# Seven products of halves in place of eight in one product of a two-MLP kernel

## The chip, the cores and the metric

The kernel runs on one NeuronCore of a Trainium2 chip. The core has five engines with queues of their own: TensorE (PE; its weight loads are shown as PEld), VectorE (DVE), ScalarE (ACT), GpSimd (POOL) and SyncE (SP), which issues most DMAs. Matmuls write into PSUM, eight banks of 512 f32 values in each of 128 partitions; everything else works in SBUF. The metric is the device time of one execution in microseconds (us); of several executions the median is told.

## What is computed

```python
# q, k, v: (4, 8, 576, 64) f32
out_up    = repeat(softmax_attention(mean of 4 rows of q, k, v), 4)   # pooled attention
out_local = softmax(q k^T / 8 where |i - j| < 4) v                    # windowed attention
x = (out_up + out_local) as (2304, 512)

h = x @ w_in                                   # first MLP, 512 -> 2048 -> 512
x = np.maximum(0.01 * h, h) @ w_out

h = x @ w_in2                                  # second MLP, 512 -> 2048 -> 512
g = np.where(h >= 1, h, np.where(h <= -1, 0.0, (h + 1) ** 2 / 4))
out = g @ w_out2                               # (2304, 512) f32
```

## The kernel before

**Numbers.** Every operand of the four MLP products is held as two f16 parts, a high one and the rest (`hi`, `lo`). A product is made of three f16 products, hi x hi, hi x lo and lo x hi, that add up in PSUM.

**Tiling.** The 2304 tokens are cut into five blocks, `BLOCKS = [512, 512, 512, 512, 256]`. A stage is one MLP m and one block b, and `ORDER` lists the ten stages. A stage of 512 tokens has 16 steps, one for each tile f of 128 columns of d_ff; the 256-token block has 8 steps with two tiles each. A step is:

- `g1`: the first product of one f (two for block 4), 4 tiles of d_model x 3 = 12 matmuls of all the block's tokens (24 of 256 columns for block 4), into one PSUM bank.
- `act_a` to `act_l`: the activation out of the bank and the split into hi and lo. In the first MLP that is `act_a` and `act_h` on ScalarE and `act_l` on VectorE; in the second `act_a`, `act_s` (ScalarE), `act_g` (VectorE, it frees the bank), `act_h` (ScalarE) and `act_l` (VectorE).
- `g2`: the second product's share of that f, 12 matmuls that add up in the stage's up to four `acc` banks over all steps. Behind the last step `fin_*` evict them, and in the second MLP a DMA writes the result.

The weights are loaded by SyncE, converted by VectorE and ScalarE, and stay in SBUF (`w1`, `w2`). The space of `w2` serves as scratch (`w` in the trace) for the attention until the second MLP's weights come. All other buffers come from one arena.

**Attention.** Batch 0 and part of batch 1 go through TensorE (`prep`, `down`, `local_p`), the remaining units of 256 tokens through VectorE (`local_d`: products and sums over windows). `ADD_PE` lists the batches for which `local_p` adds the pooled attention by an f32 matmul with the identity into the bank (L1106); for the others VectorE adds it (`xa`).

**Order.** Nothing is ordered at run time. A planner in the kernel (`Issue.run`) goes through modelled time, and gives each free engine the ready operation with the lowest key; keys come from the step an operation is due in, less a lead. Gates limit what is open: a first product may start while under two (`h_open`) are open, and a stage's `acc` banks wait for those of the stage before. `QUEUE` is how far the planner lets SyncE issue ahead of the modelled DMAs, `lat` what it takes a DMA to cost. Up to 140 us it puts matmuls of zeros (`fill`, L1675) where TensorE would stand idle in its model. The instructions then stand in each engine's queue in that order, with semaphore waits between engines.

## Time and profile before

| | |
|---|---|
| median of 3 runs | 862.63 us (861.98 to 864.24) |
| profiled execution | 868.02 us, its span 866.2 us |
| TensorE busy, matmuls | 855.9 us, 5029 records |
| VectorE, ScalarE, GpSimd busy | 551.4, 386.2, 44.4 us |
| mean granted TensorE clock | 0.997 |
| DMA | 67.69 MB |

The span goes from the first to the last instruction; the run's time has a little around it. Matmuls are pipelined: a record runs until its result has left the array, so records overlap, and the spacing of their starts tells what one costs. In the profile DVE is VectorE and so on, `bank` is PSUM, `arena` and `w` are buffers in SBUF, and `<-` goes from what is read to what is written.

### The profile page before, as it was taken

The numbers are of one execution on the slowest core, as the hardware profiler recorded it, in microseconds if no ns is written. First come the engines' busy times: TensorE is split into PE (matmuls) and PEld (weight loads), VectorE is DVE, ScalarE is ACT, GpSimd is POOL, SyncE is SP. The second block draws the span as 40 slices with busy tenths as digits, with TensorE's granted clock in tenths as the row PEclk, the third lists the DMA queues.
The fourth block names the chain that finished last, engine by engine and source line by source line (L and its number), as shares of the span: only waits on it lengthen the run. The fifth ranks groups of instructions, "written<-read, shape, count | busy, mean of one in ns | idle before, by whom it ended". The sixth has DMA issues, their size and how long they took to land.

```text
span 866.2 us, 13124 instructions
## 1 busy us (share of the span) xinstructions
PE 855.9 (99%) x5029; PEld 440.8 (51%) x5039; DVE 551.4 (64%) x975; ACT 386.2 (45%) x909; POOL 44.4 (5%) x64
## 2 busy tenths in 40 slices
PE   9998999999999999999999999999999999999998
PEld 5764555444444444444444444444444488544564
DVE  5767999899999899569959928921323211322221
ACT  5858776364444334644453223222433332433343
POOL 2201000000000033001410000000000000000000
PEclk9999999999999999999999999999999999999999
DMA  7999574647720353321751002000000010000010
GB/s 133 183 156 206 183 220 151 219 137 221 219 92 2 110 82 69 98 76 28 119 136 43 1 30 81 1 0 1 1 1 1 0 50 1 1 1 1 1 50 25
DMA packets 80365, 67.69 MB, mean 78 GB/s; under 512 B 36398, under 2 KB 70062, under 8 KB 80302
## 3 DMA queue, kind: packets, MB, share of 16 engines
q1 hardware_dynamic: 69102, 62.69, 26.9%
q0 software_dynamic: 11200, 4.15, 4.3%
q8 instruction: 40, 0.66, 0.3%
q14 instruction: 23, 0.19, 0.1%
HBM read 62.08 MB, written 4.72 MB: 77 GB/s over the span
## 4 chain that ended last, share of the span: by engine, by line
PE 81%; DVE 7%; DMA 6%; issue 2%; ACT 2%; SPq 1%; POOL 0%; DVEq 0%; POOLq 0%; ACTq 0%
PE bank L1471 38%; PE bank L1536 21%; PE bank L1548 16%; DMA w<-in_v_dram 4%; DMA arena<-in_v_dram 2%; DVE arena L1322 1%; PE bank L962 1%; PE bank L944 1%; DVE arena L1515 1%; DVE arena L1499 1%; DVE arena L1292 1%; ACT w L1070 1%; PE bank L1112 1%; PE bank L893 1%; SPq L732 1%
## 5 line engine op out<-in xcount | busy, mean ns | idle before, releaser
L1471 PE MATMUL bank<-arena,w 128*128 128x512 f16 (+1 forms) x1920 | 396.9, 358 | 0.4 <-ACT arena L915 0.3
L1471 PEld LDWEIGHTS <-w 128*128 128x128 f16 x1920 | 186.8, 98 | 183.9 <-issue 2.8
L1536 PE MATMUL bank<-arena,w 128*128 128x512 f16 (+1 forms) x960 | 198.8, 358 | 0.2
L1548 PE MATMUL bank<-w,arena 128*128 128x512 f16 x864 | 198.5, 379 | 0.4 <-ACT arena L1511 0.2
L1515 DVE SCALAR_TENSOR_TENSOR arena<-arena 128x512 f16<-128x512 f32 x144 | 99.3, 690 | 122.6 <-ACT arena L1511 122.4
L1536 PEld LDWEIGHTS <-w 128*128 128x128 f16 x960 | 92.9, 98 | 91.5 <-issue 1.2
L1499 DVE SCALAR_TENSOR_TENSOR arena<-arena,bank 128x512 f32<-128x512 f32 x72 | 49.3, 685 | 135.2 <-ACT arena L1495 135.2
L1548 PEld LDWEIGHTS <-arena 128*128 128x128 f16 x864 | 83.7, 98 | 97.9 <-issue 1.0
L1511 ACT ACTIVATE arena<-arena 128x512 f16<-128x512 f32 x144 | 90.6, 629 | 74.1 <-DVE arena L1499 72.0
L1491 ACT ACTIVATE arena<-bank,half 128x512 f32<-128x512 f32 x72 | 49.4, 686 | 132.5 <-PE bank L1471 132.5
L1487 ACT ACTIVATE arena<-bank 128x512 f32<-128x512 f32 x72 | 42.9, 595 | 141.8 <-PE bank L1471 140.2
L1495 ACT ACTIVATE arena<-arena 128x512 f32<-128x512 f32 x72 | 45.3, 629 | 2.0
L1322 DVE TENSOR_TENSOR arena<-arena 128x768 f32<-128x768 f32 (+2 forms) x60 | 41.2, 689 | 1.5
L1247 DVE TENSOR_TENSOR arena<-arena 128x1792 f32<-128x1792 f32 x20 | 40.3, 2019 | 0.5 <-DMA arena<-in_k_dram 0.4
L1255 DVE TENSOR_REDUCE arena<-arena 128x28 f32<-128x1792 f32 x20 | 40.3, 2013 | 0.0
L1292 DVE TENSOR_TENSOR arena<-arena 128x1792 f32<-128x1792 f32 x20 | 40.2, 2016 | 0.0
L607 ACT ACTIVATE w<-arena 128x512 f16<-128x512 f32 x37 | 23.2, 629 | 35.8 <-DVE arena L591 35.5
L840 POOL DMA_DIRECT2D arena<-in_q_dram x8 | 10.4, 1296 | 300.1 <-DMA arena<-in_q_dram 233.6
L640 DVE SCALAR_TENSOR_TENSOR w<-arena,w 128x512 f16<-128x512 f32 x37 | 25.4, 692 | 0.1
L1675 PE MATMUL bank<-zeros 128*128 128x512 bf16 x65 | 20.9, 418 | 3.5 <-ACT w L1099 2.0
L584 DVE SCALAR_TENSOR_TENSOR arena<-arena 128x512 int32<-128x512 int32 x33 | 22.8, 694 | 0.1
L591 DVE SCALAR_TENSOR_TENSOR arena<-arena 128x512 int32<-128x512 int32 x33 | 22.8, 693 | 0.0
(132 smaller groups left out, 628.5 us busy)
## 6 DMA issues: line engine op xcount, KB each, us to landing
arena<-in_moe_w_out_dram SPq DMA_DIRECT2D x21, 512.0 KB
arena<-in_moe_w_in_dram SPq DMA_DIRECT2D x17, 512.0 KB
w<-in_moe_w_in_dram SPq DMA_DIRECT2D x15, 512.0 KB
w<-in_moe_w_out_dram SPq DMA_DIRECT2D x11, 512.0 KB
out_dram<-arena SPq DMA_DIRECT2D x18, 256.0 KB
arena<-in_k_dram SPq DMA_DIRECT2D x23, 112.0 KB
arena<-in_v_dram SPq DMA_DIRECT2D x23, 112.0 KB
w<-in_q_dram SPq DMA_DIRECT2D x14, 144.0 KB
```

Source lines behind the costliest of these rows:

```text
L1247: nc.vector.tensor_tensor(pv(par, j0), st["q", par].ap.rearrange("p (j d) -> p j d", d=D)[:, j0:j0 + JC, :] .unsqueeze(2).to_broadcast([P, ...
L1292: nc.vector.tensor_tensor(pv(par, j0), window(st["v", par], j0, JC), sv(par)[:, j0:j0 + JC, :].unsqueeze(3).to_broadcast([P, JC, W, D]), o ...
L1322: nc.vector.tensor_tensor(out, x, y, op=ALU.add)
L1471: nc.tensor.matmul(h[:, e], a[:, f, c, :], y[:, :, c, :], start=(n == 0), stop=(n == 3 * KDM - 1),)
L1487: nc.scalar.activation(out=t, in_=st["h", p], func=AF.Prelu, scale=s_in * sg, alpha=0.01)
L1491: nc.scalar.activation(out=t, in_=st["h", p], func=AF.Relu, scale=0.5 * s_in, bias=half)
L1495: nc.scalar.activation(out=t, in_=t, func=AF.Square, scale=s_in ** -0.5)
L1499: nc.vector.scalar_tensor_tensor(out=t, in0=t, scalar=1.0 / s_in, in1=st["h", p], op0=ALU.min, op1=ALU.max)
L1511: nc.scalar.activation(out=gv(p)[0], in_=st["t", p].ap, func=AF.Copy, scale=so)
L1515: nc.vector.scalar_tensor_tensor(out=lo, in0=st["t", p].ap, scalar=so, in1=hi, op0=ALU.mult, op1=ALU.subtract)
L1536: nc.tensor.matmul(o, a, y[:, e, :], start=(first and n == 0 and c % E == 0), stop=(last and n == 2), skip_group_check=True,)
L1548: nc.tensor.matmul(st["acc"][tt], a, y[:, f, :], start=(first and n == 0), stop=(last and n == 2),)
```

## The change

The first product of the second MLP, for token blocks 2, 3 and 4 (1280 tokens), is made by the seven-product scheme of Strassen in Winograd's form. d_model, d_ff and the block's tokens are each halved. Eight products of halves would be the plain way; seven are enough when sums of halves are multiplied. With weight quarters A(row half of d_ff, half of d_model) and token quarters B(half of d_model, half of the tokens):

- `weight_sums` makes S1 to S4 of the weight quarters for each f of the lower half of d_ff (`FH` = 8 tiles), once. VectorE adds, ScalarE makes the high part, VectorE the low part. S3 takes the place of quarter 21 in `w2`; this starts when the last plain stage of the second MLP, block 1, has used its weights.
- `token_sums` makes T1 to T4 of a block in the same way.
- A step now handles a pair, f and f+8 (two pairs of tiles at once in block 4), in two banks, one for each half of the tokens, each bank holding both d_ff halves. `s1` makes three products, ScalarE copies two of them out (`m5`, `m1`), `s2` adds two more products, ScalarE copies one sum (`m53`), VectorE adds into the banks (`d0`, `d1`), `s3` adds a product, VectorE adds (`d2`, which completes the second half of the tokens), `s4` adds the last one (the first half of the tokens is complete).
- A product of halves (`prod`) is 2 tiles of d_model x 3 = 6 matmuls over half the block's tokens: 256 columns in the 512 blocks; in block 4, where E = 2 tiles go together, 12 matmuls of 128 columns.
- The activation runs as before on a bank of 512 values, now for one half of the tokens and both f. The second product (`g2_half`) is made in groups of 6 matmuls of 512 columns for one half of the tokens and one f.

Beside that, stage (1, 4), the first MLP's 256-token block, goes ahead of (2, 2); `ADD_PE` is empty; `QUEUE` is 3, and the planner's `lat` of two kinds of loads differ.

```diff
 ORDER = [
     (1, 0), (1, 1), (2, 0), (2, 1), (1, 2), (1, 3),
-    (2, 2), (1, 4), (2, 3), (2, 4),
+    (1, 4), (2, 2), (2, 3), (2, 4),
 ]
+SEVEN = (2, 3, 4)
...
-QUEUE = 2
+QUEUE = 3
...
-ADD_PE = (0,)
+ADD_PE = ()
...
-        o = ch.op("SP", DMA, load, need=(1024,), lat=1.75)
+        o = ch.op("SP", DMA, load, need=(1024,), lat=(2.3, 1.6)[which])
...
+    def half_sums(ch, n, quarter, dst, recipe, deps, need):
+        st = {}
+        ready = {}
+        def make(name, x, y, sx, sy):
+            if name == recipe[0][0] and need:
+                need[1]()
+            qx = quarter(x)
+            if y in st:
+                st[name] = b = buf(n)
+                v = b.ap[:, 0:n]
+                if len(qx.shape) == 4:
+                    v = v.rearrange("p (a b) -> p a b", a=qx.shape[2])
+                st["v" + name] = v
+                f = st["v" + y]
+                if sx > 0:
+                    nc.vector.tensor_tensor(v, qx[:, 0], f, op=ALU.subtract)
+                    nc.vector.tensor_tensor(v, v, qx[:, 1], op=ALU.add)
+                else:
+                    nc.vector.tensor_tensor(v, f, qx[:, 0], op=ALU.subtract)
+                    nc.vector.tensor_tensor(v, v, qx[:, 1], op=ALU.subtract)
+            else:
+                st[name] = b = buf(2 * n)
+                a = b.ap.rearrange("p (k x) -> p k x", k=2)
+                if len(qx.shape) == 4:
+                    a = a.rearrange("p k (a b) -> p k a b", a=qx.shape[2])
+                nc.vector.tensor_tensor(a, qx, quarter(y), op=ALU.add if sy > 0 else ALU.subtract)
+                v = st["v" + name] = a[:, 0]
+                nc.vector.tensor_tensor(v, v, a[:, 1], op=ALU.add)
...
+        def lo(name):
+            d = dst(name)
+            nc.vector.tensor_tensor(d[:, 1], st["v" + name], d[:, 0], op=ALU.subtract)
...
+            h = ch.op("ACT", t_act(n), lambda name=name: hi(name), [o])
+            ready[name] = o = ch.op(
+                "DVE", t_dve(n), lambda name=name: lo(name), [h],
...
+    def weight_sums(f, due):
...
+            s_ap[f] = {"S1": a[:, 0], "S2": a[:, 1], "S4": a[:, 2], "S3": quarter("21")}
...
+        s_ready[f] = half_sums(
+            ch, HD, quarter, lambda nm: s_ap[f][nm],
+            (("S1", "21", "22", 1, 1), ("S2", "11", "S1", -1, 1), ("S4", "12", "S2", 1, -1),
+             ("S3", "11", "21", 1, -1)),
+            s_after[f], (words, make))
...
+    def token_sums(b, due):
...
+        t_ready[b] = half_sums(
+            ch, 2 * n, quarter, lambda nm: t_ap[b][nm],
+            (("T1", "12", "11", 1, -1), ("T2", "22", "T1", 1, -1), ("T4", "21", "T2", 1, -1),
+             ("T3", "22", "12", 1, -1)),
+            x2[b].ready, (KDM * tokens(b), make))
...
-                           need=(QBB * P,), lat=1.85)
+                           need=(QBB * P,), lat=1.95)
...
+        def prod(p, t, j, w, y, first=False):
+            o = part(p, t, j)
+            for e in range(E):
+                n = 0
+                for c in range(2):
+                    a = w(E * p + e).rearrange("p s (c n) -> p s c n", c=2)
+                    for i, k in ((0, 0), (0, 1), (1, 0)):
+                        nc.tensor.matmul(
+                            o[:, e], a[:, i, c], y[:, k, c, :],
+                            start=first and e == 0 and n == 0, stop=n == 5,
+                            skip_group_check=True,
+                        )
+                        n += 1
...
+        def s1(p, i):
+            sch.step = max(sch.step, i)
+            h_open[0] += 2
+            for t in range(2):
+                st["h", (p, t)] = banks.get(True)
+            prod(p, 1, 0, ws("S1"), t_ap[b]["T1"], True)
+            prod(p, 0, 1, wq(0, 0), xq(0, 0), True)
+            prod(p, 0, 0, wq(0, 1), xq(1, 0))
+        def side(p, nm):
+            return st[nm, p].ap[:, 0:E * NH].rearrange("p (a n) -> p a n", a=E)
+        def copy(p, nm, t, j):
+            st[nm, p] = buf(E * NH)
+            nc.scalar.copy(side(p, nm), part(p, t, j))
+        def s2(p):
+            prod(p, 1, 0, ws("S4"), xq(1, 1))
+            prod(p, 0, 1, ws("S2"), t_ap[b]["T2"])
+        def d0(p):
+            nc.vector.tensor_tensor(part(p, 0, 0), part(p, 0, 0), side(p, "m1"), op=ALU.add)
+        def d1(p):
+            nc.vector.tensor_tensor(part(p, 1, 0), part(p, 0, 1), side(p, "m53"), op=ALU.add)
+        def s3(p):
+            prod(p, 0, 1, ws("S3"), t_ap[b]["T3"])
+        def d2(p):
+            nc.vector.tensor_tensor(part(p, 1, 1), part(p, 0, 1), side(p, "m5"), op=ALU.add)
+        def s4(p):
+            prod(p, 0, 1, wq(1, 1), t_ap[b]["T4"])
...
+            def copied(nm, t, j, dep, p=p, key=key):
...
+            o1 = sch.add(
+                "PE", fn=lambda p=p, i=i: s1(p, i),
+                deps=x.ready + [w_ready[m, 0, f] for f in fs] + sr["S1"] + [tr["T1"]],
+                key=float(i), banks=2,
+                gate=lambda i=i: h_open[0] <= 2 and i < low_step[0] + LAGMAX, **unit(3),
+            )
+            m5 = copied("m5", 1, 0, o1)
+            m1 = copied("m1", 0, 1, o1)
+            o2 = sch.add("PE", fn=lambda p=p: s2(p),
+                         deps=[m5, m1, tr["T2"]] + sr["S4"] + sr["S2"], key=i + 0.2, **unit(2))
+            m53 = copied("m53", 1, 0, o2)
+            a0 = summed(d0, "m1", [o2])
+            a1 = summed(d1, "m53", [m53])
+            o3 = sch.add("PE", fn=lambda p=p: s3(p), deps=[a0, a1, tr["T3"]] + sr["S3"],
+                         key=i + 0.4, **unit(1))
+            a2 = summed(d2, "m5", [o3])
+            o4 = sch.add("PE", fn=lambda p=p: s4(p),
+                         deps=[a2, tr["T4"]] + [w_ready[m, 0, f + FH] for f in fs],
+                         key=i + 0.6, after=(x.s.done, t_buf[b].done) if p == PH - 1 else (),
+                         **unit(1))
+            halves.append((p, 1, i + 1, i + 2.5, a2))
+            halves.append((p, 0, i, i + 4.1, o4))
+        for p, t, i, key, o1 in halves:
+            fs = [E * p + e for e in range(E)]
+            ol = act((p, t), i, o1)
+            for j in range(2):
+                first = p == j == 0 and t == 1
+                og2 = sch.add(
+                    "PE", 3 * NACC // 2 * t_mm(512) * E,
+                    lambda p=p, t=t, j=j, i=i: g2_half(p, t, j, i),
+                    [ol, og2] + [w_ready[m, 1, f + FH * j] for f in fs],
...
     for m, b in ORDER:
+        if m == 2 and b in SEVEN:
+            if not s_ready:
+                for f in range(FH):
+                    weight_sums(f, first[m, b] + 2.0 * (f // per_step(b)))
+            token_sums(b, first[m, b])
         stage(m, b)
```

The places where the order differs, as far as a later step rests on it. On TensorE, in the second MLP's block 2, before: a first product of 12 matmuls into one bank, and then a second product of 12. `w_61` is the second MLP's weights, `bank_66` and the like are PSUM banks, and the arena holds the tokens and the activations.

```order
L1471 LDWEIGHTS w_61
L1471 MATMUL bank_65<-arena,w_61 128x512 [waits DVE_49]
...
L1471 MATMUL bank_65<-arena,w_61 128x512
L1548 LDWEIGHTS arena [waits Activation_49]
L1548 MATMUL bank_68<-w_61,arena 128x512
```

After, in the same block, the third pair: the end of its `s1` (L1626) with the second-product group (L1696) behind it, then `s2` into two banks, a second-product group, and the start of `s3`.

```order
L1626 LDWEIGHTS w_61
L1626 MATMUL bank_66<-arena,w_61 128x256
L1696 LDWEIGHTS arena [waits Activation_49]
L1696 MATMUL bank_70<-w_61,arena 128x512
...
L1626 MATMUL bank_69<-arena 128x256 [waits Activation_49]
...
L1626 MATMUL bank_66<-arena 128x256 [waits Activation_49]
...
L1696 LDWEIGHTS arena
L1696 MATMUL bank_70<-w_61,arena 128x512
...
L1626 LDWEIGHTS w_61
L1626 MATMUL bank_66<-arena,w_61 128x256 [waits DVE_49]
```

Where one first product and one second product of 12 matmuls took turns, a piece of 6 to 18 matmuls takes turns with a group of 6, and pieces that go on in a pair wait for ScalarE (`Activation`) or VectorE.

On VectorE in the same block, before, the two operations of the activation chain, L1499 and L1515, stand alone:

```order
L1499 SCALAR_TENSOR_TENSOR arena<-arena,bank_69 128x512 [waits PE_49,Activation_49]
L1515 SCALAR_TENSOR_TENSOR arena<-arena 128x512 [waits Activation_49]
L1499 SCALAR_TENSOR_TENSOR arena<-arena,bank_67 128x512 [waits PE_49,Activation_49]
L1515 SCALAR_TENSOR_TENSOR arena<-arena 128x512 [waits Activation_49]
L1499 SCALAR_TENSOR_TENSOR arena<-arena,bank_65 128x512 [waits PE_49,Activation_49]
```

After, one pair: the three adds into the banks (L1666, L1669, L1676) and the two activation chains (L1721, L1737).

```order
L1666 TENSOR_TENSOR bank_65<-bank_65,arena 128x256 [waits PE_49,Activation_49]
L1669 TENSOR_TENSOR bank_64<-bank_65,arena 128x256 [waits DVE_49,Activation_49]
L1676 TENSOR_TENSOR bank_64<-bank_65,arena 128x256 [waits DVE_49,PE_49]
L1721 SCALAR_TENSOR_TENSOR arena<-arena,bank_64 128x512 [waits DVE_49,Activation_49]
L1737 SCALAR_TENSOR_TENSOR arena<-arena 128x512 [waits Activation_49]
L1721 SCALAR_TENSOR_TENSOR arena<-arena,bank_65 128x512 [waits PE_49,Activation_49]
L1737 SCALAR_TENSOR_TENSOR arena<-arena 128x512 [waits Activation_49]
```

Three operations that wait for TensorE and for the copies of ScalarE have come between the chains.

On TensorE near 27 us, before: the f32 matmul of the pooled attention (L1106) in front of each group of the windowed one (L1112), with fill matmuls (L1675) between.

```order
L1106 MATMUL bank_66<-arena,ident 128x256 [waits Activation_49]
L1112 MATMUL bank_66<-w_61 64x64 [waits DMAHW0_49]
L1112 MATMUL bank_66<-w_61 64x64 [waits DMAHW1_49]
L1112 MATMUL bank_66<-w_61 64x64 x6
L1675 LDWEIGHTS zeros
L1675 MATMUL bank_63<-zeros 128x512
...
L1106 MATMUL bank_65<-arena,ident 128x256 [waits DVE_49]
```

After, the same place: L1238 is the windowed attention's product, L1964 the fill.

```order
L1964 LDWEIGHTS zeros
L1964 MATMUL bank_63<-zeros 128x512
L1238 MATMUL bank_70<-w_61 64x64 [waits DMAHW0_49,Activation_49]
L1238 MATMUL bank_70<-w_61 64x64 [waits DMAHW1_49]
L1238 MATMUL bank_70<-w_61 64x64 x6
L1964 LDWEIGHTS zeros
L1964 MATMUL bank_63<-zeros 128x512
L1238 MATMUL bank_65<-w_61 64x64 [waits DVE_49,Activation_49]
```

L1106 has gone, and its place is taken by a fill matmul or nothing; what it added is now added by VectorE.

## Rows read from the trace of the kernel before

**Rows 1.** The page, parts 1 and 2: busy time, and slices in tenths.

```profile
PE 855.9 (99%) x5029; PEld 440.8 (51%) x5039; DVE 551.4 (64%) x975; ACT 386.2 (45%) x909; POOL 44.4 (5%) x64
...
PEclk9999999999999999999999999999999999999999
```

**Rows 2.** The page, part 4: the chain that ended last, by engine and line.

```profile
PE 81%; DVE 7%; DMA 6%; issue 2%; ACT 2%; SPq 1%; POOL 0%; DVEq 0%; POOLq 0%; ACTq 0%
PE bank L1471 38%; PE bank L1536 21%; PE bank L1548 16%; DMA w<-in_v_dram 4%; DMA arena<-in_v_dram 2%; DVE arena L1322 1%; PE bank L962 1%; PE bank L944 1%; DVE arena L1515 1%; DVE arena L1499 1%; DVE arena L1292 1%; ACT w L1070 1%; PE bank L1112 1%; PE bank L893 1%; SPq L732 1%
```

**Rows 3.** The chain in time, two late pieces: start, length (us), what.

```profile
505.43 2.59 PE bank L1471 x12
...
718.95 2.62 PE bank L1471 x24
```

**Rows 4.** The chain in order of time, between 40 and 80 us.

```profile
44.23 7.73 DMA w<-in_v_dram
...
65.61 8.23 DMA w<-in_v_dram
77.94 3.64 PE bank L1471 x12
```

**Rows 5.** Groups by shape, weight loads: xcount, busy us, mean ns, idle.

```profile
L1471 PEld LDWEIGHTS <-w 128*128 128x128 f16 x1920 | 186.8, 98 | 183.9 <-issue 2.8 <-DVE w L577 0.3
...
L944 PEld LDWEIGHTS bank<-ident,w 72*72 72x72 f32 x64 | 5.4, 115 | 2.1 <-ACT w L915 0.2
```

**Rows 6.** Timeline at 336 us: start us, length us, engine, line, operation.

```profile
336.27 0.46 PEld L944 LDWEIGHTS bank<-ident,arena 72*72 72x72 f32 x4
...
336.48 0.42 PE L944 MATMUL bank<-ident,arena 72*72 72x72 f32 x4
...
336.73 0.38 PE L1548 MATMUL bank<-w,arena 128*128 128x512 f16 x1
```

**Rows 7.** Timeline, second MLP, block 2: the chain behind a first product.

```profile
684.85 2.75 PE L1548 MATMUL bank<-w,arena 128*128 128x512 f16 x12
685.05 0.69 ACT L1491 ACTIVATE arena<-bank,half 128x512 f32<-128x512 f32 x1 [2.45 <-PE bank L1471]
685.77 0.63 ACT L1495 ACTIVATE arena<-arena 128x512 f32<-128x512 f32 x1
686.43 0.69 DVE L1499 SCALAR_TENSOR_TENSOR arena<-arena,bank 128x512 f32<-128x512 f32 x1 [3.10 <-ACT arena L1495]
...
687.81 0.69 DVE L1515 SCALAR_TENSOR_TENSOR arena<-arena 128x512 f16<-128x512 f32 x1 [0.69 <-ACT arena L1511]
```

**Rows 8.** Groups by shape: 256-column copy and add out of a bank.

```profile
L780 ACT ACTIVATE w<-bank 128x256 f32<-128x256 f32 x16 | 6.1, 384 | 0.6 <-PE bank L767 0.6
...
L1342 DVE TENSOR_TENSOR arena<-bank,arena 128x256 f32<-128x256 f32 x4 | 1.5, 420 | 1.1 <-PE bank L1328 1.1
```

**Rows 9.** Timeline, the end of the program.

```profile
856.51 2.75 PE L1548 MATMUL bank<-w,arena 128*128 128x512 f16 x12
...
858.81 0.63 ACT L1511 ACTIVATE arena<-arena 128x512 f16<-128x512 f32 x1 [0.75 <-DVE arena L1499]
...
859.49 3.06 PE L1548 MATMUL bank<-w,arena 128*128 128x512 f16 x12 [0.23 <-ACT arena L1511]
```

**Rows 10.** Stretches (us): length, busy us of PE, PEld, DVE, ACT, POOL, clock, DMA.

```profile
460.00:515.00 55.00, 55.00 (x285) 26.62 (x284) 41.60 (x59) 17.64 (x40) 0.26 (x1) 1.00 0.00 1
515.00:560.00 45.00, 45.00 (x210) 20.42 (x209) 37.50 (x47) 13.37 (x24) 0.25 (x1) 1.00 0.18 53
560.00:610.00 50.00, 50.00 (x234) 22.66 (x232) 10.87 (x15) 11.94 (x20) 0.00 (x0) 1.00 0.00 0
```

**Rows 11.** Groups by shape: the f32 matmuls that add the pooled attention.

```profile
L1106 PE MATMUL bank<-arena,ident 128*128 128x256 f32 x16 | 5.4, 418 | 0.3 <-ACT arena L970 0.2 <-ACT w L780 0.2
```

**Rows 12.** Timeline of TensorE at 27 us.

```profile
26.85 0.69 PE L1106 MATMUL bank<-arena,ident 128*128 128x256 f32 x2 [0.16 <-ACT arena L970]
...
28.09 0.61 PE L1675 MATMUL bank<-zeros 128*128 128x512 bf16 x2
```

128 lines of the change are left out of this document (117 added, 11 removed).

## The prediction

> **What bounds the kernel now.** I read the page's first two parts first [rows 1]. TensorE is busy 855.9 us, 99% of the span, VectorE 551.4 and ScalarE 386.2, and the granted clock stands at 9 in every slice, the 2.4 GHz level. A busy share says little of pipelined matmuls, so the chain of work that ended last came next [rows 2]: 81% of it is TensorE, and its three long lines are the matmuls of the two MLPs (L1471 the first product, L1536 and L1548 the second). In order of time [rows 3] these pieces stand end to end: 12 matmuls of 512 columns take 2.59 us, 24 of 256 columns 2.62 us. So a matmul costs its columns, 216 ns and 109 ns from start to start, and no step waits for another. From about 78 us to the end the time is the sum of TensorE's work; before that the chain runs through DMAs of v [rows 4]. A change pays by the columns that it takes from TensorE after 78 us, less every gap that it opens there.
>
> The profiled execution took 868.0 us (span 866.2, 1.8 around it), 5.4 above the median of 862.6. The terms below are differences in that execution, and I take their sum off the median too.
>
> **Columns removed.** Token blocks 2 and 3 (512 tokens each) and 4 (256 tokens) of the second MLP change. Before, the first product of a 512 block is 16 steps of 12 matmuls of 512 columns, so two blocks are 384 x 0.216 = 82.9 us; block 4 is 192 matmuls of 256 columns, 192 x 0.109 = 20.9 us. Together 103.9 us. Afterwards a pair of column tiles (f and f+8) takes seven products of 6 matmuls over half the tokens each. Blocks 2 and 3: 2 x 8 pairs x 42 = 672 matmuls of 256 columns, 672 x 0.109 = 73.2 us. The second product keeps its 480 matmuls of 512 columns, now in groups of six.
>
> Block 4 becomes 4 pairs x 84 = 336 matmuls of 128 columns, each with a weight load of its own. No f16 matmul of 128 columns stands in the trace. From below: 216 less 109 ns for 256 columns is 0.418 ns a column, which gives 55.5 ns and 18.6 us in all. From above: a weight load of this form is recorded as 98 ns [rows 5], and if the matmuls come no faster than that, it is 32.9 us. I take 55.5, because the nearest row speaks for it: four f32 transposes of 72 columns take 0.25 us (336.48 to 336.73), 62 ns each, although each has a weight load of its own [rows 6], recorded as 115 ns [rows 5]. The recorded length of a load is a latency, not a spacing, and a load with a matmul can be issued every 62 ns. So the first product falls from 103.9 to 73.2 + 18.6 = 91.8 us, 12.1 less; with the upper price it would be 106.1, 2.2 more.
>
> Here the Trainium skill speaks against the change. Its page "TensorE: Matmul & The Clock Gate", section "Back-to-back issue gap", says that a stream of weight loads and matmuls sustains about 81 ns per matmul at 128 columns. By that, block 4 takes 27.2 us and the first product falls by 3.5 us alone. The same sentence has about 131 ns at 512 columns, where this trace has 216, so the trace disagrees with it there.
>
> **Hand-offs inside a pair.** This is the new risk. A pair is four pieces in a row, and each of three joints waits for other engines: piece one (three products), two copies on ScalarE; piece two (two products), a copy and two adds; piece three, an add; piece four. At each joint of a steady pair the order has one group of six second-product matmuls for TensorE, 6 x 0.216 = 1.30 us. What the joints need, by rows: 0.20 us from the start of the next group on TensorE to that of ScalarE (684.85 to 685.05) [rows 7]; 0.38 for a 256-column copy out of a bank and 0.42 for a 256-column add that reads one [rows 8]; 0.03 from ScalarE to VectorE (685.77 + 0.63 to 686.43) [rows 7]; 0.05 from ScalarE to TensorE (858.81 + 0.63 to 859.49) [rows 9]. Joint one is at most 0.20 + 2 x 0.38 + 0.05 = 1.01; joint two, with the first add beside the copy, 0.20 + 0.38 + 0.03 + 0.42 + 0.05 = 1.08; joint three 0.20 + 0.42 + 0.05 = 0.67. All are under 1.30 as long as neither engine is in the middle of something. An add that writes into a bank has no row; between 0.27 (a 512-column operation, 0.69, less the 256-column one) and 0.69, joint two stays within 0.93 and 1.35, that is 0 to 0.05 us of waiting in each of 20 pairs. I price it as the add that reads a bank.
>
> What is queued there: a pair lasts 42 x 0.109 + 24 x 0.216 = 9.8 us. ScalarE has 3 copies and two chains of three operations in it (3 x 0.38 + 2 x 1.95 = 5.0 us), VectorE 3 adds and 4 operations of 0.69 (4.0 us). The chain after a piece runs 3.65 us, from 684.85 to 687.81 + 0.69 [rows 7]. The next pair's first copy comes 1.30 + 18 x 0.109 + 0.20 = 3.5 us after the last piece: only ScalarE's last operation of that chain can stand in its way, and joint one has 0.3 us to spare for it; joints two and three find both engines free. So a steady pair costs nothing. The pattern is broken in block 2, where the second pair's joint one has one product in front of it (6 x 0.109 = 0.65 against 1.01), and at block 3, where token sums still run on VectorE. I put 1.0 us for all such places; the bounds are 0 and rival 1.
>
> **Work added beside.** Weight sums: for each of 8 tile pairs 12 VectorE operations, 2 of 512 and 10 of 256 columns, 2 x 0.69 + 10 x 0.42 = 5.6 us, 45 us in all; block 2's token sums, 2 of 1024 and 10 of 512 columns, are some 10 us. These 55 us must be done by about 610 us, when block 2 starts. From 460 to 610 us VectorE is idle for 13.4 + 7.5 + 39.1 = 60 us [rows 10], and the order ends them ten steps (10 x 5.2 us) ahead. The sums of blocks 3 and 4 (15 us) and 60 adds (25 us) come after 610, where VectorE has only this stage's own chains beside them. ScalarE gets 96 short operations of 0.38 and 8 of 0.63, 42 us. All of it lies beside TensorE. The 256-token stage of the first MLP moves one stage ahead, and with it its windowed attention on VectorE and its loads on SyncE's queue; the last operation is now queued four steps, some 20 us, ahead of that stage. Without that cover TensorE would wait for it.
>
> **The front.** With ADD_PE empty, 12 f32 matmuls leave TensorE, the 8 long ones with 5.4 us of busy time [rows 11], and 12 adds of up to 0.42 us come to VectorE. They stand between 26 and 50 us, where TensorE is filled up with idle matmuls (L1675 in [rows 12]) and the chain goes on into v's DMAs, 7.7 and 8.2 us each, up to 74 us [rows 4]: worth nothing. The order has 19 more fill matmuls, 4.1 us, 14 of them behind the first MLP step; on SyncE one weight load goes ahead of a q and k load, with the same bytes. Where the fills stand TensorE would mostly be idle. I take 0, with 4 us either way: all the fills paid on one side, the removed matmuls given back on the other.
>
> **The end.** Before, the 12 matmuls ahead of the last group don't cover the 3.65 us chain: that group should start at 856.51 + 2.59 = 859.10 and starts at 859.49, and it lasts 3.06 us in place of 2.75 [rows 9], 0.7 us in all. Now 48 second-product matmuls, 10.4 us, stand behind the last piece: -0.7 us. What follows, two evictions and their DMAs, is the same.
>
> **Sum.** -12.1 + 1.0 + 0 - 0.7 = -11.8 us: 856.2 in the profiled execution's own time, 850.8 us as a median.
>
> **Rivals.**
> 1. The joints stall (slower). If at joint two of every pair an operation of 0.63 on ScalarE and one of 0.69 on VectorE stand ahead, it needs 1.08 + 1.32 = 2.40, 1.10 over its cover; over 20 pairs that is 22 us, and the time is 872. It decides from (11.8 + 1.0) / 20 = 0.6 us a pair on. For it: the spare time is only 0.2 us, and a chain of 3.65 us reaches up to the next pair's joint one. Against it: by the lengths above those operations fall elsewhere.
> 2. Weight loads bind at 128 columns. At 98 ns block 4 gives back 14.3 us: 865.1. The timeline [rows 6] speaks against it. By the page's 81 ns it would be 8.6 us, 859.4.
> 3. The front gets longer by the fills and the moved load: 855. Its opposite: 847.
> 4. VectorE is late. The order queues about 20 us per four steps of 20.7 on it ahead of the moved stage. At 10% longer operations it is 10 us late, within the 20 us of cover; 5 us beyond it make 856.
> 5. The change doesn't do what it says: the order holds 1008 matmuls of the new shapes for 576, so nothing is left for this.
>
> **How the numbers follow.** A measurement of this kernel tells some 0.3%, 2.6 us, from no change. The forecast (847 to 855) has 0.68. Joints: 0.05 for a small loss (855 to 860), 0.05 for a decisive one. Weight loads bind: 0.07, of which 0.02 slower, 0.02 within the bound at 98 ns, 0.03 near the page's price and within the bound. Front longer, front shorter, VectorE late: 0.05 each, all faster. So faster 0.68 + 0.05 + 0.15 = 0.88, same 0.05, slower 0.07. The range leaves out the decisive stall and the full weight loads above, and a front that gives back more than all removed matmuls below: 845 to 860.
>
> **What would show it.** Right: 256-column matmuls 109 ns apart and 128-column ones near 56; less than 2 us of idle TensorE after 90 us; the last 48 matmuls without a wait; the first MLP step near 60 us. Wrong: waits of the new lines for copies or adds of over 0.6 us a pair, 128-column matmuls 80 ns or more apart, or TensorE's closed stretch starting later than at 78 us.

## The result and the profile after

The changed kernel takes 853.59 us (median of 4 runs, 852.79 to 854.13) against 863.43 for the kernel before on the same chip. The ratio is 0.9877, 95% interval 0.985 to 0.9903: 10.6 us less (8.4 to 13.0). The two medians by themselves lie 9.8 us apart; the ratio on record, which is used from here on, is not their quotient. The forecast was 850.8, 11.8 less, with a range of 845 to 860.

The page of the kernel after, parts 1, 2 and 4 (busy time, slices in tenths, the chain by engine and by line), answers to [rows 1, 2]:

```profile
PE 844.0 (99%) x5466; PEld 466.4 (55%) x5466; DVE 638.5 (75%) x1179; ACT 419.1 (49%) x1013; POOL 43.9 (5%) x64
...
PEclk9999999999999999999999999999999999999999
...
PE 92%; DVE 6%; ACT 1%; issue 0%; ACTq 0%; DVEq 0%
PE bank L1597 30%; PE bank L1758 20%; PE bank L1696 11%; PE bank L1770 10%; PE bank L1626 10%; PE bank L1964 3%; PE bank L893 1%; PE bank L1178 1%; PE bank L1088 1%; PE bank L1019 1%; PE bank L1070 1%; PE bank L1238 1%; DVE arena L735 1%; DVE arena L744 1%; PE bank L1221 1%; DVE arena L1737 1%
```

VectorE has 87 us more to do and ScalarE 33, TensorE 12 less. The chain no longer holds a DMA: the v loads of [rows 4] have left it, and 3% of it are fills (L1964). Its 6% of VectorE are new in kind: among their lines are L735 and L744, the sums, and they lead to the waits below.

Line numbers are those of the new kernel: L1597 is the plain first product, L1626 the seven-product pieces, L1696 and L1770 the second MLP's second product (in halves, and plain), L1758 the first MLP's, L1964 the fill. The groups by shape (xcount | busy us, mean ns | idle us and what ended it), beside [rows 5]:

```profile
L1626 PE MATMUL bank<-arena,w 128*128 128x256 f16 x384 | 49.3, 273 | 0.4 <-DVE bank L1669 0.4
...
L1626 PE MATMUL bank<-arena 128*128 128x256 f16 x288 | 36.7, 273 | 0.1
L1626 PE MATMUL bank<-arena,w 128*128 128x128 f16 x192 | 12.7, 219 | 0.0
L1626 PE MATMUL bank<-arena 128*128 128x128 f16 x144 | 9.3, 219 | 0.0
```

The counts are those of the working: 672 matmuls of 256 columns, 336 of 128. Their mean lengths say nothing of cost, the spacing does. TensorE's timeline (start us, length us, engine, line, operation) where block 3 hands over to block 4 shows it, against [rows 6, 7]:

```profile
791.83 1.47 PE L1626 MATMUL bank<-arena 128*128 128x256 f16 x12
793.14 1.46 PE L1696 MATMUL bank<-w,arena 128*128 128x512 f16 x6
794.43 0.82 PE L1626 MATMUL bank<-arena,w 128*128 128x256 f16 x6
795.09 1.46 PE L1696 MATMUL bank<-w,arena 128*128 128x512 f16 x6
796.38 0.82 PE L1626 MATMUL bank<-arena,w 128*128 128x256 f16 x6
797.04 1.46 PE L1696 MATMUL bank<-w,arena 128*128 128x512 f16 x6
798.33 0.83 PE L1626 MATMUL bank<-arena 128*128 128x128 f16 x12
799.00 1.17 PE L1626 MATMUL bank<-arena,w 128*128 128x128 f16 x18
```

Twelve matmuls of 256 columns take 1.31 us, six of 512 take 1.29, and 12 of 128 take 0.67, 56 ns each, although each brings a weight load, as recorded still 98 ns long. Pieces and groups follow each other without a gap.

The waits of TensorE, its only three (line waited for, us in all, times, longest):

```profile
PE bank L1964 <- DVE half L449: 1.2, 1, 1.2
PE bank L1758 <- DVE arena L1737: 1.1, 3, 0.6
PE bank L1626 <- DVE bank L1669: 0.4, 1, 0.4
```

Measured by spacing (a start minus the start before it, less 216, 109 or 56 ns by shape) the gaps from 300 us on, but for 1.5 us around attention matmuls that both kernels have, sum up to 3.3 us: 1.55 in stage (1,3), the first MLP's last block of 512 tokens, and 1.73 in the seven-product stages. The first kind stands here in TensorE's timeline; the number in brackets is the idle time and what ended it:

```profile
574.43 0.38 PE L1758 MATMUL bank<-arena,w 128*128 128x512 f16 x1
575.07 2.53 PE L1758 MATMUL bank<-arena,w 128*128 128x512 f16 x11 [0.25 <-DVE arena L1737]
```

The two starts lie 0.64 us apart in place of 0.22; two more such places follow, at 581 and 592 us. L1737 is the low part of the first MLP's activation, which VectorE makes between the weight sums. The matmuls have 512 columns, so this is stage (1,3); the moved stage (1,4) has 256, begins at 604.9 us and has no gap.

At the end the last second products run through, where [rows 9] had a wait: in the timeline from 840 us, the last row of TensorE's matmuls holds 28 of the last 48 matmuls in one piece.

```profile
840.83 6.21 PE L1696 MATMUL bank<-w,arena 128*128 128x512 f16 x28
```

### The profile page after: what moved, and what is told of

The parts are those of the page before. It is cut to its first block, busy times and chain, and to the rows that moved or that the text cites. A ratio compares the mean times of both kernels' runs of the same rounds, so it can differ in the third digit from the quotient of the medians.

```text
span 851.3 us, 14356 instructions
## 1 busy us (share of the span) xinstructions
PE 844.0 (99%) x5466; PEld 466.4 (55%) x5466; DVE 638.5 (75%) x1179; ACT 419.1 (49%) x1013; POOL 43.9 (5%) x64
## 4 chain that ended last, share of the span: by engine, by line
PE 92%; DVE 6%; ACT 1%; issue 0%; ACTq 0%; DVEq 0%
PE bank L1597 30%; PE bank L1758 20%; PE bank L1696 11%; PE bank L1770 10%; PE bank L1626 10%; PE bank L1964 3%; PE bank L893 1%; PE bank L1178 1%; PE bank L1088 1%; PE bank L1019 1%; PE bank L1070 1%; PE bank L1238 1%; DVE arena L735 1%; DVE arena L744 1%; PE bank L1221 1%; DVE arena L1737 1%
## 5 line engine op out<-in xcount | busy, mean ns | idle before, releaser
L1597 PE MATMUL bank<-arena,w 128*128 128x512 f16 (+1 forms) x1344 | 285.4, 364 | 0.0
L1597 PEld LDWEIGHTS <-w 128*128 128x128 f16 x1344 | 130.3, 98 | 134.2 <-issue 1.2
L1758 PE MATMUL bank<-arena,w 128*128 128x512 f16 (+1 forms) x960 | 199.0, 358 | 1.1 <-DVE arena L1737 1.1
L1737 DVE SCALAR_TENSOR_TENSOR arena<-arena 128x512 f16<-128x512 f32 x144 | 98.6, 687 | 72.8 <-ACT arena L1733 72.5
L1758 PEld LDWEIGHTS <-w 128*128 128x128 f16 x960 | 93.1, 98 | 90.3 <-issue 2.1
L1696 PE MATMUL bank<-w,arena 128*128 128x512 f16 x480 | 115.2, 379 | 0.2
L1770 PE MATMUL bank<-w,arena 128*128 128x512 f16 x384 | 88.2, 379 | 0.0
L1721 DVE SCALAR_TENSOR_TENSOR arena<-arena,bank 128x512 f32<-128x512 f32 x72 | 49.0, 682 | 38.9 <-ACT arena L1717 38.8
L1696 PEld LDWEIGHTS <-arena 128*128 128x128 f16 x480 | 46.1, 98 | 42.5 <-DVE arena L1737 1.2
L1626 PE MATMUL bank<-arena,w 128*128 128x256 f16 (+1 forms) x576 | 62.0, 255 | 0.4 <-DVE bank L1669 0.4
L1770 PEld LDWEIGHTS <-arena 128*128 128x128 f16 x384 | 36.8, 98 | 43.2 <-issue 1.4
L1626 PEld LDWEIGHTS <-w 128*128 128x128 f16 x576 | 49.1, 98 | 12.6 <-issue 0.7
L1626 PE MATMUL bank<-arena 128*128 128x256 f16 (+1 forms) x432 | 46.0, 255 | 0.1
L1626 PEld LDWEIGHTS <-arena 128*128 128x128 f16 x432 | 36.8, 98 | 10.9 <-issue 0.6
```

Source lines behind the costliest of these rows:

```text
L1597: nc.tensor.matmul(h[:, e], a[:, f, c, :], y[:, :, c, :], start=(n == 0), stop=(n == 3 * KDM - 1),)
L1626: nc.tensor.matmul(o[:, e], a[:, i, c], y[:, k, c, :], start=first and e == 0 and n == 0, stop=n == 5, skip_group_check=True,)
L1696: nc.tensor.matmul(st["acc"][t * NACC // 2 + k], a, y[:, f, :], start=(p == j == e == n == 0), stop=(p == PH - 1 and j == 1 and e == E - 1 ...
L1721: nc.vector.scalar_tensor_tensor(out=t, in0=t, scalar=1.0 / s_in, in1=st["h", p], op0=ALU.min, op1=ALU.max)
L1737: nc.vector.scalar_tensor_tensor(out=lo, in0=st["t", p].ap, scalar=so, in1=hi, op0=ALU.mult, op1=ALU.subtract)
L1758: nc.tensor.matmul(o, a, y[:, e, :], start=(first and n == 0 and c % E == 0), stop=(last and n == 2), skip_group_check=True,)
```

## The experiments

Each ratio is to runs of the kernel before on the same chip; the changed kernel's is 0.9877. Most edits let the planner order the whole program anew, so a run can differ in places that its edit doesn't touch; only runs 7 and 8 lengthen operations in an order that stays.

**1. All but the seven products.**

```
-SEVEN = (2, 3, 4)
+SEVEN = ()
```

> Everything of the change but the seven products: the 256-token stage of the first MLP one place earlier, no f32 matmuls for the pooled attention, the other queue depth and DMA costs of the planner; all first products plain. My account (the columns carry the gain, the front is worth nothing): 860 to 863 us, within 0.3% of before, and no waits for the first MLP's low parts (L1737) around 575 to 592 us, because the weight sums that crowd VectorE there are gone. Rival (the front or the moved stage carries several us, as the first MLP step at 55.7 us in place of 59.9 in the profiles suggests): 855 to 859 us.

Measured: 861.17 us, ratio 0.9957 (0.9941 to 0.9972), 3.7 us under before. The range of my account held the median, but the interval leaves out a ratio of 1: what this run keeps of the change, the front, the moved stage and the end together, is worth 2.4 to 5.1 us. The first MLP step starts at 55.62 us, as in the changed kernel (55.68) and not as before (59.91). The waits for L1737 are gone, so they belong to the sums. Between this trace and that of the changed kernel the last matmul moves from 854.90 to 846.66 us: the seven products gain 8.2 us, which is about 11.9 by their columns less 3.3 of gaps, and not the 11.8 that I had put down to them and the end.

**2. The old order of stages.**

```
-    (1, 4), (2, 2), (2, 3), (2, 4),
+    (2, 2), (1, 4), (2, 3), (2, 4),
```

> The change with the old order of stages: (2,2) ahead of (1,4) again, everything else kept. My account (the stage was moved so that the weight sums find room on VectorE): the 55 us of sums now have to be done some 20 us earlier, in a stretch where VectorE had about 21 us free, so TensorE waits: 856 to 866 us, with waits of the seven-product lines for L744 or of the first MLP for its attention. Rival (the move does nothing for the sums, the planner fills the gaps in any order): within 1 us of the changed kernel, 852 to 855 us.

Measured: 880.52 us, ratio 1.018 (1.0158 to 1.0202). Worse than either said. TensorE's waits, the two longest (line numbers are three lower here):

```profile
PE bank L1594 <- DVE arena L1795: 10.3, 1, 10.3
PE bank L1451 <- DVE arena L1445: 7.8, 1, 7.8
```

One wait of 10.3 us for VectorE's low part of an eviction and one of 7.8 for the windowed attention: with the sums due ahead of stage (1,4) VectorE is late with both. Without the moved stage a gain of 10.6 us becomes a loss of 15.6.

**3. The planner told what a sum costs.** 

```
-            o = ch.op("DVE", 2 * t_dve(n) if of_sum else t_dve(2 * n) + t_dve(n),
+            o = ch.op("DVE", 2 * t_dve(n) + 0.13 if of_sum else t_dve(2 * n) + t_dve(n) + 0.13,
```

> The change with the planner told that a sum costs 0.13 us more on VectorE: in the trace of after an operation that reads what the one before it wrote starts 0.45 us behind it, an independent one 0.34. My account (the three waits of 0.6 to 1.0 us at 575 to 592 us come from sums that run longer than planned and push the activation's low part late): the waits of L1758 for L1737 fall from 1.6 us to under 0.5, and the time to 852 to 853 us, 1 us under the changed kernel. Rival (VectorE has no room left there, busy 98% from 460 to 580 us, and a better plan can't make any): the waits stay or move, 853 to 855 us.

The row that it rests on, in VectorE's timeline of the kernel after: L729 reads what L728 wrote, and starts 0.45 us behind it; L725 reads nothing of L729's, and starts 0.35 behind.

```profile
572.74 0.42 DVE L728 TENSOR_TENSOR arena<-arena,w 128x256 f32<-128x256 f32 x1
573.19 0.43 DVE L729 TENSOR_TENSOR arena<-arena,w 128x256 f32<-128x256 f32 x1
573.54 0.42 DVE L725 TENSOR_TENSOR arena<-w,arena 128x256 f32<-128x256 f16 x1
```

Measured: 851.95 us, ratio 0.9849 (0.9825 to 0.9873). The three waits are gone. The stretches of this run (length, then busy us of PE, PEld, DVE, ACT, POOL) show that VectorE is as full as in the kernel after (19.52 and 17.75 us there) and TensorE without idle time (19.75 and 19.20 there):

```profile
560.00:580.00 20.00, 20.00 (x97) 9.47 (x96) 19.50 (x46) 9.03 (x21) 0.00 (x0) 1.00 0.00 1
580.00:600.00 20.00, 20.00 (x96) 9.23 (x95) 17.76 (x41) 9.72 (x21) 0.00 (x0) 1.00 0.00 1
```

So the rival (no room left) falls. It was the place of the sums, planned 0.13 us too short each, not their amount. The time alone, 1.6 us under the changed kernel, is less than the two intervals tell apart; the gaps in the traces, 1.8 us in place of 3.3, carry it. In the kernel after, VectorE has room right behind these waits: it is busy for 8.6 of 44 us.

```profile
600.00:620.00 20.00, 20.00 (x151) 14.59 (x150) 5.16 (x8) 6.85 (x12) 0.00 (x0) 1.00 0.00 1
620.00:644.00 24.00, 24.00 (x222) 21.52 (x221) 3.46 (x5) 6.13 (x10) 0.00 (x0) 1.00 0.00 1
```

**4. A fourth block.** SEVEN takes in block 1, and the order becomes

```
+    (1, 0), (1, 1), (1, 2), (2, 0), (1, 3), (1, 4),
+    (2, 1), (2, 2), (2, 3), (2, 4),
```

> Seven products for block 1 of the second MLP too (four of five blocks), with the order of stages (1,0) (1,1) (1,2) (2,0) (1,3) (1,4) (2,1) (2,2) (2,3) (2,4), so that all first-MLP stages still come ahead of the seven-product ones. My account by columns alone: another 192 matmuls of 512 columns (41.5 us) become 336 of 256 (36.6 us), 4.9 us less: 848 to 850 us. Rival (VectorE becomes the bound: three first-MLP stages have to find their attention done before the first stage of the second MLP gives it time, and the 55 us of sums come no later than before): TensorE waits for VectorE before 610 us and the time is over 856 us.

Measured: 894.57 us, ratio 1.0355 (1.0328 to 1.0381). My account fell, the rival stands. TensorE's longest wait:

```profile
PE bank L1451 <- DVE arena L1445: 15.2, 2, 9.1
```

15.2 us are waits for VectorE's windowed attention (L1454 in the changed kernel), the four longest waits for ScalarE add 13.5, and the mean granted clock is 0.977 against 1.000. In this order VectorE doesn't deliver the attention in time. Whether the 4.9 us of columns could be had in another order isn't shown: the run changes the blocks and the order together.

**5. The front as before.** ADD_PE = (0,), QUEUE = 2 and the old lat values, with seven products and the new order.

> The change (seven products, new order of stages) with the settings of the front as before: the f32 matmuls of the pooled attention on TensorE for batch 0, queue depth 2, the old DMA costs of the planner. My account after the first runs (the front settings are worth 3.7 us, the seven products the rest): ratio 0.992 to before, about 857.5 us, with the first MLP step (L1597) near 60 us. The prediction's account (the front is worth nothing): the time of the changed kernel, ratio 0.988, about 853.6 us, with the first step near 56 or 60 us alike.

**6. Only the f32 matmuls back.**

```
-ADD_PE = ()
+ADD_PE = (0,)
```

> The change with the f32 matmuls of the pooled attention back on TensorE for batch 0, nothing else. The prediction's account (they stand where TensorE is filled up with idle matmuls, and cost nothing): within 0.7 us of the changed kernel, ratio 0.987 to 0.989; what the front gains then comes from the order of the DMAs. Rival (they delay the windowed attention of the first blocks, whose banks they fill): the front's gain of 3.7 us is theirs, ratio 0.992, about 857.5 us, the first MLP step near 60 us.

Measured: 857.85 us, ratio 0.9924 (0.9909 to 0.9938) for the front as before; 859.29 us, ratio 0.9936 (0.9924 to 0.9948) for the f32 matmuls alone. Against 0.9877 these are 4.1 and 5.1 us. So the front's gain is that of the f32 matmuls; queue depth and DMA costs bring nothing that can be told. The prediction's 0 is refuted; its bound below, the removed matmuls given back, is what happened. The first MLP step stands at 61.40 and 61.00 us. The groups by shape of the second run, up to 61 us:

```profile
L1964 PE MATMUL bank<-zeros 128*128 128x512 bf16 x61 | 20.1, 418 | 1.2 <-DVE half L449 1.2
...
L1232 PE MATMUL bank<-arena,ident 128*128 128x256 f32 x16 | 5.2, 405 | 0.0
...
L1232 PE MATMUL bank<-arena,ident 128*128 128x64 f32 x8 | 1.5, 273 | 0.0
```

L1232 is the f32 matmul (L1106 before): 24 of them, 5.87 us from start to start. The changed kernel has 64 fills ahead of its first step, this one 61. So 5.9 us of work went in and 0.7 us of fills out, and the first step came 5.3 us later. The last matmul comes 5.3 us later too, but not by the front alone: block 2 starts 4.5 us later, and a joint of 1.8 us at 666 us, which the changed kernel doesn't have, adds to it. The front's part is thus nearer 4 us, as in run 5. The stretches of the same run say why nothing swallowed it:

```profile
20.00:40.00 20.00, 20.00 (x249) 13.84 (x250) 16.62 (x49) 17.61 (x83) 4.24 (x8) 1.00 0.90 156
40.00:55.00 15.00, 15.00 (x184) 11.14 (x182) 11.64 (x38) 9.92 (x38) 1.55 (x4) 1.00 1.02 192
```

TensorE is never idle there, fills included, in this run as in the changed kernel. The fills are fixed in its queue; they don't shrink when something else takes longer. Why the planner puts in only three fewer wasn't tried.

**7 and 8. Joint two made longer,** on VectorE and on ScalarE.

```
         def d1(p):
+            nc.vector.tensor_scalar(side(p, "m53"), side(p, "m53"), 1.0, None, op0=ALU.mult)
```

```
             st[nm, p] = buf(E * NH)
+            for _ in range(3 if nm == "m53" else 0):
+                nc.scalar.copy(side(p, nm), part(p, t, j))
```

> The change with one more VectorE operation of 256 columns ahead of the second add of every pair (the copied sum times 1.0 in place; 20 pairs), that is in joint two. From the trace of after: the first add starts 0.27 us after the covering group, the second 0.53 behind it, and the next piece 0.49 behind that, 1.29 us against a cover of 1.30, so an operation of 0.2 to 0.45 us is paid in full: 4 to 9 us slower than the changed kernel, and 20 waits of the seven-product line for L1670. The prediction's account (joint two needs 1.08, 0.22 to spare, because the first add lies beside the copy): 0 to 4.6 us. Rival (the queues hide more than the records show): no change.

> The change with the copy in joint two made four times by ScalarE in place of once (20 pairs, some 0.3 us more each time). From the trace of after: the copy starts 0.85 us after the piece began, when its first product is complete, and not at its end, so it is done 0.9 us before the second add needs it: 0.9 to 1.1 us more cost 0 to 0.2 us a pair, 0 to 4 us. The prediction's account (the copy waits for the whole piece and has 0.22 us to spare): 0.7 to 0.9 us a pair, 14 to 18 us slower than the changed kernel.

Joint two of the fourth pair in the timeline of the kernel after: piece two, copy, covering group, the two adds, piece three.

```profile
694.78 1.47 PE L1626 MATMUL bank<-arena 128*128 128x256 f16 x12
695.63 0.37 ACT L1658 COPY arena<-bank 128x256 f32<-128x256 f32 x1 [1.44 <-PE bank L1626]
...
696.09 1.46 PE L1696 MATMUL bank<-w,arena 128*128 128x512 f16 x6
696.36 0.43 DVE L1666 TENSOR_TENSOR bank<-bank,arena 128x256 f32<-128x256 f32 x1 [1.98 <-PE bank L1626]
696.89 0.43 DVE L1669 TENSOR_TENSOR bank<-bank,arena 128x256 f32<-128x256 f32 x1
...
697.38 0.82 PE L1626 MATMUL bank<-arena,w 128*128 128x256 f16 x6
```

Measured: 855.37 us (ratio 0.9898, 0.9883 to 0.9913) with the operation on VectorE, 1.8 us over the changed kernel; 859.79 us (0.9947, 0.9934 to 0.996) with the copies, 6.0 over. Seven: the operation lengthens the way from the first add to the second by 0.13 us (0.66 for 0.53), and a steady pair now has a gap of 0.12 at piece three. So joint two had 0.01 us to spare. The total by itself decides nothing, since it lies in the prediction's 0 to 4.6 us too; the gap in every steady pair does. The total fell below the 4 to 9 us expected, because I had taken the operation's length for its price: it runs while the second add would have waited for the first. Eight, same place in its timeline:

```profile
697.80 0.37 ACT L1658 COPY arena<-bank 128x256 f32<-128x256 f32 x1 [1.44 <-PE bank L1626]
...
698.20 1.18 ACT L1660 COPY arena<-bank 128x256 f32<-128x256 f32 x3
...
698.52 0.43 DVE L1668 TENSOR_TENSOR bank<-bank,arena 128x256 f32<-128x256 f32 x1 [1.97 <-PE bank L1626]
...
699.42 0.43 DVE L1671 TENSOR_TENSOR bank<-bank,arena 128x256 f32<-128x256 f32 x1 [0.46 <-ACT arena L1660]
699.90 0.81 PE L1626 MATMUL bank<-arena,w 128*128 128x256 f16 x6 [0.19 <-DVE bank L1671]
```

Three copies add 1.2 us (0.40 each, more than I took), and the second add comes 0.37 later, so the copy had 0.83 us to spare and not 0.22. Piece three of a steady pair now starts 0.35 us late, in 17 pairs 6.0 us, which is the whole loss and more than the 0 to 4 of my account. The prediction's account of this joint (14 to 18 us) is refuted: the copy leaves when its own product is complete, in the middle of the piece.

**9 and 10. Fewer fills,** on top of run 3: FILL = 56 and FILL = 20 in place of 140.

> The version with the corrected VectorE cost (851.95 us in its own runs), and in it no fill matmuls of zeros planned beyond 56 us in place of 140: 64 of them for 94. My account (TensorE is never idle after 20 us in the trace, so its queue runs behind the plan and a fill there is work like any other, which is also why the f32 matmuls of the pooled attention cost 5 us): up to 30 x 0.216 = 6.5 us less, 845.5 to 849 us. Rival, the prediction's (the fills stand where TensorE would be idle): the same waits without the fills, 851 to 853 us, or more if the clock falls in the gaps.

> The same, and no fills planned beyond 20 us: 39 of them for 94. My account (TensorE's sum is the bound of the front): another 25 x 0.216 = 5.4 us, the first MLP step near 49 us and 840 to 845 us. Rival (ahead of 56 us the front hangs on DMAs, VectorE and ScalarE, and only there are the fills free): the first MLP step stays at 55 to 57 us, TensorE has idle stretches of some 5 us in all between 20 and 56 us, and the time is that of the run with 64 fills, or longer if the granted clock falls below 0.95 there.

Measured: 855.49 us (ratio 0.9888, 0.9872 to 0.9905) and 857.24 us (0.9909, 0.9893 to 0.9925), 3.5 and 5.3 us over run 3. My account fell in both. With 64 fills the first step stays at 55.68, TensorE is idle for 3.8 us between 62 and 90, and the granted clock between 70 and 80 is 0.83; yet block 2 starts at 642.7 us, against 642.8 in run 3. So up to there the 30 fills neither cost nor bring anything, as the rival said. The 3.5 us are lost in block 3, where the new order has joint one wait for copies that ScalarE makes behind its activation chain:

```profile
742.73 2.50 PE L1626 MATMUL bank<-arena 128*128 128x256 f16 x11 [2.15 <-ACT arena L1658]
```

These matmuls start 213 ns apart in place of 109, and the granted clock from 742 to 746 us is 0.57. From the start of block 2 to the last matmul this run takes 4.1 us more than run 3. With 39 fills the stretches read:

```profile
20.00:40.00 20.00, 17.38 (x263) 13.19 (x260) 17.49 (x52) 16.07 (x79) 5.12 (x7) 1.00 0.88 165
40.00:50.00 10.00, 5.54 (x55) 4.34 (x56) 8.21 (x25) 7.15 (x28) 0.00 (x0) 0.53 0.88 201
...
62.00:70.00 8.00, 8.00 (x53) 5.14 (x50) 6.88 (x19) 6.88 (x33) 1.33 (x3) 0.50 1.28 216
```

TensorE is idle for 2.6 us of 20 and then for 4.5 of 10; the clock falls to the 1.2 GHz level (0.53, 0.50) and stays there while TensorE is busy all the time from 50 to 70 us. The first step comes at 66.65, and block 2 starts 5.8 us later than in run 3. So the 25 fills between 20 and 56 us are worth more than they take, the 30 behind them nothing either way, and yet real work put among the former is paid (run 6). Neither account had the whole of this. Whether the f32 matmuls would be free if fills gave way to them wasn't tried.

**11. Two blocks.** SEVEN = (2, 3), block 4 plain and ahead of them.

> Seven products for blocks 2 and 3 alone; block 4 of the second MLP is plain and goes ahead of them: stages (1,4) (2,4) (2,2) (2,3). It tests the price of the 128-column matmuls by the time and not by the trace. My account (they cost 55.5 ns each, so block 4 gains 20.9 - 18.6 = 2.3 us by seven products): 2.3 us slower than the changed kernel, less up to 1.6 us for the waits of VectorE, which gets a stage of 256 tokens more time for the sums: 854 to 856 us, ratio 0.989 to 0.992. Rival (81 ns, the rule on back-to-back issue in the page on TensorE's matmuls of the Trainium skill): block 4 loses 6.3 us by seven products, and without them the time is 846 to 848 us, ratio 0.98.

Measured: 859.89 us, ratio 0.9942 (0.9926 to 0.9959), 5.6 us over the changed kernel. The rival is out: at 81 ns this kernel would have been the faster one. My size was off too. TensorE's waits of the pieces:

```profile
PE bank L1626 <- DVE bank L1676: 2.3, 3, 0.8
PE bank L1626 <- DVE bank L1669: 1.3, 2, 0.9
...
PE bank L1626 <- ACT arena L1658: 0.9, 1, 0.9
```

By spacing its gaps are 6.8 us against 3.3, and the end, with 512 tokens to evict in place of 256, is 0.8 longer. 2.3 for the columns, 3.5 and 0.8 make 6.6, about what the spans show (857.7 against 851.3). One stretch says where most of the gaps come from (length, busy us of PE, PEld, DVE, ACT):

```profile
695.00:720.00 25.00, 21.40 (x153) 14.70 (x151) 24.33 (x57) 17.60 (x40) 0.00 (x0) 1.00 0.06 23
```

The sums take the place of a weight quarter that the last plain stage still needs, and here that stage stands right before block 2. So they run beside the first pairs, VectorE is full, and the joints wait behind them; I had thought that the plain stage would give them time.

**12. The first add taken out of joint two,** on top of run 3.

```
-            a0 = summed(d0, "m1", [o2])
...
-            o3 = sch.add("PE", fn=lambda p=p: s3(p), deps=[a0, a1, tr["T3"]] + sr["S3"],
+            o3 = sch.add("PE", fn=lambda p=p: s3(p), deps=[a1, tr["T3"]] + sr["S3"],
...
+            a0 = summed(d0, "m1", [o4])
...
-            halves.append((p, 0, i, i + 4.1, o4))
+            halves.append((p, 0, i, i + 4.1, a0))
```

> The version with the corrected VectorE cost (851.95 us, ratio 0.9849 in its own runs), and the first add of every pair (d0) made behind the last piece of the pair in place of joint two, so that joint two waits for the copy and one add. My account (joint two is 0.27 + 0.53 + 0.49 = 1.29 us against 1.30 of cover, the first add being 0.53 of it): it falls to 0.8 us; a steady pair still costs nothing more or less, and only where the cover is shorter, at the second pair of block 2 (0.6 us) and in block 3 (0.25 us), is something gained: 0.5 to 1 us, 851 to 851.5 us. Rival (the add is now ahead of the activation of the first half of the tokens, half a us later in each pair, and the second product of that half waits): 20 pairs of up to 0.5 us, 852 to 862 us.

Measured: 850.38 us, ratio 0.9827 (0.9795 to 0.986), the fastest. Its gaps by spacing are 0.1 us. Beside the idle start, TensorE's list of waits holds one row:

```profile
PE bank L1964 <- DVE half L449: 1.2, 1, 1.2
PE bank L1070 <- ACT w L1196: 0.2, 1, 0.2
```

That is 1.6 us under run 3, more than the 0.5 to 1 expected: run 3's smaller gaps (0.13 to 0.29 us at five places, three of them waits for a copy) went too. The rival (second products wait for the later add) doesn't show. Changed kernel, run 3 and run 12 have gaps of 3.3, 1.8 and 0.1 us and times of 853.6, 852.0 and 850.4: the gaps account for the times within 0.2 us. Their ratios, 0.9877, 0.9849 and 0.9827, have intervals that overlap from one to the next, so that the order of the three rests on the gaps.

## Why the prediction was right, step by step

**The sign and the size** held, but three terms were wrong: gaps of 2.3 us more than forecast, and 3.0 us gained in the front that were put at nothing. That they offset each other is luck.

**Columns: right.** The removed products cost 103.9 us by the rows; the added ones run for 92.4 us from start to start, 0.4 of it gaps: 11.9 less, where 12.1 was forecast. The one open price, 128 columns, came out at 56 ns against 55.5 taken; four f32 transposes, each with its own load, had been the right nearest row. The Trainium skill ("TensorE: Matmul & The Clock Gate", "Back-to-back issue gap") has 81 ns sustained with weight loads, and 56 and 216 for isolated matmuls; this trace has the latter two in streams of loads and matmuls.

**Joints: a steady pair costs nothing, as said, but by 0.01 us and not 0.22.** Of the parts of joint two, the copy was charged to the end of the piece, though it starts 0.46 us before the covering group (695.63 against 696.09), and the two adds were taken as if only one lay on the path. They are a row: 0.27 + 0.53 + 0.49 = 1.29 us against 1.30 of cover. The two mistakes nearly cancelled. The broken places, priced at 1.0 us, were 1.7: 0.60 at block 2's second pair, 0.25 at block 3's start, and four of 0.15 to 0.28, three of them second products that wait for an activation. The first two places had been named, but the pair in block 2 for the wrong joint: its joint one has no gap (18 matmuls from 654.00 to 655.96), and its joint two waits, because operations of the activation chain stand ahead of the adds on VectorE. That is rival 1's mechanism, in one place.

```profile
658.01 0.68 DVE L1721 SCALAR_TENSOR_TENSOR arena<-arena,bank 128x512 f32<-128x512 f32 x1
...
659.62 0.82 PE L1626 MATMUL bank<-arena,w 128*128 128x256 f16 x6 [0.44 <-DVE bank L1669]
```


**VectorE late: the step that failed.** The working had 20 us of cover for the moved stage and 60 us of room for 55 us of sums [rows 10], let all of it lie beside TensorE, and looked for a delay at the moved stage alone. That stage came through without a gap; but 0.13 us more per sum than planned pushed the low part of the activation late at three steps of the stage ahead of it, (1,3), 1.55 us. It was to be a rival that costs 5 us or nothing, and it cost a third of that, at a place that the working didn't look at. Run 3 shows it. Nor did the sums have to be done by 610 us: with the moved stage ahead of it, block 2 starts at 644.

**The front: mis-sized, 0 forecast, some 3 us measured** (run 1's 3.7, of which 0.7 are the end; the interval is 2.4 to 5.1). I read from the chain [rows 4] that the v loads bound the front, and from the fills that TensorE had room [rows 12]. Putting the f32 matmuls back cost 5.1 us (run 6), some 1 of it in later stages; their busy time is 5.4 us [rows 11]. The sign set for it, a first MLP step near 60 us, failed as well: it came at 55.68. The chain showed what ended last; it did not show that TensorE's queue, real work and fills together, was as long (never idle from 20 to 55 us in the kernel after and in run 6).

**The end: -0.7 was right in size but is no part of the seven products.** Run 1, with plain products, has no wait there either: its order leaves 36 second-product matmuls behind the last first product.

Put together: -11.9 + 3.3 - 3.7 = -12.3 (run 1's 3.7 holds the end already), against -10.6 (8.4 to 13.0) measured. The 1.7 between them lie within the interval, and no run settles them. The profiled execution of before lay 5.4 us above its median, with a stretch at a clock of 0.83 between 70 and 80 us, so its trace tells less of the front than runs 1, 5 and 6 do.

## What to carry to other kernels

A scheme that saves products pays by TensorE's columns only as far as each hand-off fits under work of another kind; lay the cover and the chain of the joint beside each other, add for add, and check which operations are in a row, because a joint of 1.29 us under 1.30 looks the same in the list of waits as one of 0.8. When a new load is put on an engine that is off the critical path, look at what stands behind it in that queue, and correct the planner's costs from a trace of the real operations. Fill matmuls are no free room just because they compute nothing: here real work put among them was paid, taking away those between 20 and 56 us cost 5.3 us, and taking away those behind brought nothing. And compare a run's trace with its base up to the place of the edit and behind it: run 9 lost its 3.5 us some 650 us behind the fills that it left out.

## What the runs showed of the hardware that had not been expected

- Two VectorE operations of 256 f32 columns start 0.35 us apart when independent and 0.45 when the second reads what the first wrote; two adds on PSUM banks, the second waiting for the first's semaphore, 0.53. A third operation put between those two cost 0.13 us, though it is recorded as 0.28 (run 7).
- The end of a matmul piece isn't what releases its reader: ScalarE started to copy the first of a piece's two products 0.46 us before the piece gave way to the next group.
- In run 10 the granted clock was 1.00 from 20 to 40 us, with TensorE idle for 2.6 us of it, 0.53 from 40 to 50, with 4.5 us idle, and 0.50, the 1.2 GHz level, from 50 to 70, with TensorE shown as busy throughout.
